# One adaLN transformer block on one Trainium2 core: a hand-set order for all engines, transposed attention output, modulation on the activations, K tiles of 112

## The chip, the cores and the metric

The kernel runs on one core of one Trainium2 chip. A core has five engines with a queue of instructions each: TensorE (PE in the profile; PEld is its weight load), VectorE (DVE), ScalarE (ACT), GpSimd (POOL) and SyncE (SP, which issues the DMA transfers). The engines here take up their instructions in the order of their queues (in VectorE's timeline of after, further down, a copy whose input was ready at 10.26 us waits behind other work until 11.7). The metric is the time of one execution on the device in microseconds (us). The profile gives the clock that TensorE was granted, as a share of full speed; in one kernel, e11 below, the span went from 210.8 us at a mean of 1.0 to 222.1 us at 0.927. A run is called slow when it is over 1.5% above the fastest of its kernel. Comparisons use fast runs.

## The reference, cut to what matters

S = 2048 tokens, D = 448, 16 heads of 28, MLP width 1792, bf16. Each token attends to 8 keys: itself and those 2, 4, ..., 14 positions back.

```python
sa, ca, ga, sb, cb, gb = silu(c) @ w_mod            # six vectors of 448
h = layernorm(x) * (1 + ca) + sa
q, k, v = h @ wqkv                                  # 16 heads of 28
logits = q . k[pos - 2*w], w = 0..7, masked below 0 # scale 28**-0.5
x = x + ga * ((softmax(logits) @ v) @ wo)
h = layernorm(x) * (1 + cb) + sb
x = x + gb * (gelu(layernorm(h) @ w1 + b1) @ w2 + b2)
```

As keys and queries differ by even numbers, both kernels treat even and odd tokens as two sequences of 1024 with a plain window of 8.

## The kernel before

The framework orders the instructions: the program states them stage by stage, and the framework's scheduler fills each engine's queue, with extra "order" edges where the program asks for them. Features are split into K tiles of 128 rows, the last one 64 real rows, a row of ones for the bias, and zeros up to 128. The attention output has queries on partitions, so it must be divided and then transposed:

```python
# attention_block: 18 blocks of 114 queries against 121 keys
pv  = 4 matmuls lhsT=hT[:, kt, k0:k0+BK], rhs=Wv[:, kt, :]        # V of the block
for half in range(2):                                            # 16 logit matmuls, K = 28
    nc.tensor.matmul(lt[0:BK, rr, ...], lhsT=kT[32*r:32*r+DH, ft, k0:k0+BK],
                     rhs=qT[32*r:32*r+DH, ft, q0:q0+BQ], tile_position=(32*r, 0))
    nc.scalar.activation(out=et_v[...], in_=lt[...], func=ACT.Exp, ...)
nc.vector.tensor_tensor(out=et, in0=et, in1=mask_rest, op=ALU.mult)
for h in range(H):                                               # et is the stationary side
    nc.tensor.matmul(po[0:BQ, h, :], lhsT=et[0:BK, h, :], rhs=vb[0:BK, h, :])   # 28 + a ones column
nc.vector.reciprocal(out=rden, in_=po[0:BQ, :, DH])
nc.vector.tensor_tensor(out=on, in0=po[..., 0:DH], in1=rden, op=ALU.mult)
for kt in range(KT):                                             # four transposes
    nc.tensor.transpose(out=pt[:, kt, :], in_=on[...], identity=ident[...])
nc.scalar.copy(out=oT[...], in_=pt[...])
# ... cut ...
# start: the modulation is folded into the weights
ca1_col = 1 + (silu(c) @ w_mod)[ca];  Wqk = wqkv * ca1_col;  Wv = wqkv * ca1_col
for ch in range(3):                                              # the bias sa @ wqkv
    4 matmuls lhsT=sa_pad[:, kt, :], rhs=wqkv_st[:, kt, ch*D:(ch+1)*D]
# ... cut ...
# order of the program
phases = [(range(0, 5), [0]), (range(5, 9), [1, 2]), (range(9, 14), [3, 4]),
          (range(14, 16), [5]), (range(16, 18), [6, 7])]         # attention blocks, MLP tile pairs
```

An MLP tile pair is 256 tokens: 56 W1 matmuls with 256 columns, Gelu, 28 W2 matmuls with 448 columns. Phases alternate attention (Exp on ScalarE) and MLP (Gelu), as each change of function costs a table load (1.28 us in the trace).

The softmax here doesn't subtract the row's maximum and nothing guards it: scores larger than these inputs give would overflow.

## Time and profile before

| | before |
|---|---|
| time, median of the runs (lowest to highest) | 238.4 us (237.66 to 239.23, four runs) |
| profiled span, mean granted clock | 234.2 us, 0.973 |
| TensorE, VectorE, ScalarE, GpSimd busy | 87%, 65%, 45%, 23% |
| start of the first QK matmul; end of QK for the first 512 tokens | 17.0 us; 25.4 us |
| TensorE time of the attention (V, logits, output, transposes) | 51.5 us |

The end of QK is taken as the start of its last matmul.

This is the profile page of before, first its span and busy times, then the rows of 40 slices for TensorE's busy share (9 is 90% or more) and for its granted clock (tenths of full speed), then the chain of waits by engine:

```profile
span 234.2 us, 4226 instructions
...
PE 204.8 (87%) x1712; PEld 130.6 (56%) x1712; DVE 151.4 (65%) x367; ACT 104.3 (45%) x139; POOL 54.4 (23%) x93
...
PE   0669988799978699989799998999998999899892
...
PEclk9997997999999999999999999799999999999998
...
PE 55%; DVE 23%; ACT 7%; POOL 6%; DMA 4%; issue 2%; SPq 1%; POOLq 0%; DVEq 0%; ACTq 0%
```

TensorE bounds the kernel. One caution for the clock: its record begins with the first change, at 13.6 us in before and 6.4 us in after, and the page counts the time before that as full speed. The spacing of matmuls says otherwise: before's bias matmuls (448 columns, 9.3 to 13.6 us) start 374 ns apart, where matmuls of 448 columns later start 189 ns apart. So the mean clocks quoted here leave out a slow start.

The next view is the timeline of TensorE in one attention block of before (start, duration of the group, engine, line, operation, out<-in, and in brackets the wait before it with what ended it):

```profile
97.49 0.32 PE L351 MATMUL lt<-qT,kT 28*121 28x114 bf16 x4
97.80 0.93 PE L383 MATMUL pw<-wo_s,oT 128*128 128x448 bf16 x4
98.67 0.44 PE L351 MATMUL lt<-qT,kT 28*121 28x114 bf16 x12
99.04 0.97 PE L340 MATMUL pv<-Wv,hT 128*121 128x448 bf16 x4
100.00 0.43 PE L351 MATMUL lt<-qT,kT 28*121 28x114 bf16 x8
100.36 0.40 PE L340 MATMUL pv<-Wv,hT 128*121 128x448 bf16 x1
100.83 0.43 PE L351 MATMUL lt<-qT,kT 28*121 28x114 bf16 x8
101.18 0.78 PE L340 MATMUL pv<-Wv,hT 128*121 128x448 bf16 x3
102.66 1.01 PE L366 MATMUL po<-vbuf_94,et 121*114 121x29 bf16 x16 [0.70 <-DVE et L361]
```

The output group (po) takes 0.87 us from start to start (15.6 us for 18 blocks).

Third, the start of before in the same view: the bias matmuls (pbias) and, last, the first QK group (pq), both after waits:

```profile
9.27 4.55 PE L259 MATMUL pbias<-wqkv_st,sa_pad 128*65 128x448 bf16 x12 [0.69 <-DMA wqkv_st<-in_A_wqkv_dram]
...
16.98 1.44 PE L198 MATMUL pq<-hT,Wqk 128*128 128x512 bf16 x3 [0.79 <-DVE hT L191]
```

Last, three groups of the page (count, then total busy us and mean ns of one): these weight loads of 114 and 121 columns take 132 to 136 ns each.

```profile
L366 PEld LDWEIGHTS <-et 121*114 121x114 bf16 x288 | 17.2, 133 | 7.4 <-DVE et L361 6.0
...
L351 PEld LDWEIGHTS <-kT 28*121 28x121 bf16 x288 | 11.1, 132 | 10.4 <-issue 9.6
...
L340 PEld LDWEIGHTS <-hT 128*121 128x121 bf16 x72 | 8.8, 136 | 3.4 <-issue 0.3
```

### The profile page before, as it was taken

The numbers are of one execution on the slowest core, as the hardware profiler recorded it, in microseconds if no ns is written. First come the engines' busy times: TensorE is split into PE (matmuls) and PEld (weight loads), VectorE is DVE, ScalarE is ACT, GpSimd is POOL, SyncE is SP. The second block draws the span as 40 slices with busy tenths as digits, with TensorE's granted clock in tenths as the row PEclk, the third lists the DMA queues.
The fourth block names the chain that finished last, engine by engine and source line by source line (L and its number), as shares of the span: only waits on it lengthen the run. The fifth ranks groups of instructions, "written<-read, shape, count | busy, mean of one in ns | idle before, by whom it ended". The sixth has DMA issues, their size and how long they took to land.

```text
span 234.2 us, 4226 instructions
## 1 busy us (share of the span) xinstructions
PE 204.8 (87%) x1712; PEld 130.6 (56%) x1712; DVE 151.4 (65%) x367; ACT 104.3 (45%) x139; POOL 54.4 (23%) x93
## 2 busy tenths in 40 slices
PE   0669988799978699989799998999998999899892
PEld 0433454365354376557686655787754675575660
DVE  5694979799978771578765557777556743666101
ACT  2324285325123158287357317655723364742230
POOL 8498000121112320023340003124202310213000
PEclk9997997999999999999999999799999999999998
DMA  6769980000001111001102200101112110200102
GB/s 203 218 200 331 351 271 3 0 0 0 3 0 22 22 28 22 3 0 25 22 0 48 78 3 0 22 3 22 27 22 78 25 22 3 78 13 9 25 0 78
DMA packets 17766, 13.37 MB, mean 57 GB/s; under 512 B 9042, under 2 KB 16851, under 8 KB 17748
## 3 DMA queue, kind: packets, MB, share of 16 engines
q1 hardware_dynamic: 17748, 13.12, 19.1%
q8 instruction: 13, 0.21, 0.4%
q14 instruction: 5, 0.04, 0.1%
HBM read 9.18 MB, written 1.84 MB: 47 GB/s over the span
## 4 chain that ended last, share of the span: by engine, by line
PE 55%; DVE 23%; ACT 7%; POOL 6%; DMA 4%; issue 2%; SPq 1%; POOLq 0%; DVEq 0%; ACTq 0%
PE pq L198 8%; PE po L366 5%; PE pw L383 4%; PE pv L340 3%; ACT hm L420 3%; PE lt L351 3%; DVE x_all L385 3%; DMA wqkv_st<-in_A_wqkv_dram 3%; DVE et L361 2%; POOL x1p_ring L393 2%; ACT et L357 2%; PE pbias L259 2%; DVE on L370 2%; DVE w_s L330 1%; PE pt L374 1%
## 5 line engine op out<-in xcount | busy, mean ns | idle before, releaser
L416 PEld LDWEIGHTS <-w_s 128*128 128x128 bf16 x448 | 43.2, 98 | 10.2 <-issue 3.2
L198 PE MATMUL pq<-hT,Wqk 128*128 128x512 bf16 x128 | 33.2, 406 | 5.6 <-ACT qT L202 2.0
L357 ACT ACTIVATE et<-lt 121x912 bf16<-121x912 f32 x36 | 32.0, 936 | 6.5 <-PE lt L351 5.6
L393 POOL TENSOR_TENSOR x1p_ring<-x_all,gbb_bc 128x448 f32<-128x448 bf16 x16 | 16.7, 1044 | 75.0 <-DVE x_all L385 72.5
L449 PEld LDWEIGHTS <-hm 128*128 128x128 bf16 x196 | 18.3, 98 | 15.4
L198 PEld LDWEIGHTS <-Wqk 128*128 128x128 bf16 x128 | 12.9, 102 | 22.8 <-issue 11.6
L376 ACT COPY oT<-pt 128x456 bf16<-128x456 bf16 (+1 forms) x18 | 9.7, 540 | 30.3 <-PE pt L374 30.2
L366 PEld LDWEIGHTS <-et 121*114 121x114 bf16 x288 | 17.2, 133 | 7.4 <-DVE et L361 6.0
L361 DVE TENSOR_TENSOR et<-et,mask_rest 121x1824 bf16<-121x1824 bf16 x18 | 19.6, 1099 | 2.5 <-ACT et L357 2.4
L340 PE MATMUL pv<-Wv,hT 128*121 128x448 bf16 x72 | 19.2, 370 | 0.1
L351 PEld LDWEIGHTS <-kT 28*121 28x121 bf16 x288 | 11.1, 132 | 10.4 <-issue 9.6
L351 PE MATMUL lt<-qT,kT 28*121 28x114 bf16 x288 | 15.4, 231 | 1.4 <-ACT et L357 0.8
L202 ACT CAST qT<-pq 128x512 bf16<-128x512 f32 x16 | 9.4, 586 | 14.7 <-PE pq L198 14.7
L383 PE MATMUL pw<-wo_s,oT 128*128 128x448 bf16 x64 | 15.0, 357 | 0.7 <-ACT oT L376 0.6
L385 DVE TENSOR_TENSOR x_all<-pw,x_all 128x448 bf16<-128x448 f32 x16 | 9.9, 618 | 6.7 <-PE pw L383 6.6
L204 DVE CAST kT<-pq 128x512 bf16<-128x512 f32 x16 | 10.9, 682 | 4.3 <-PE pq L198 4.2
L370 DVE TENSOR_TENSOR on<-po,rden 114x448 bf16<-114x448 f32 x18 | 11.0, 613 | 0.2
L340 PEld LDWEIGHTS <-hT 128*121 128x121 bf16 x72 | 8.8, 136 | 3.4 <-issue 0.3
L368 DVE RECIPROCAL rden<-po 114x16 f32<-114x16 f32 x18 | 4.6, 254 | 9.2 <-PE po L366 9.1
L420 ACT ACT_TABLE_LOAD x5 | 6.4, 1283 | 6.7 <-PE p_1015 L416 6.6
L374 PE MATMUL pt<-ident,on 114*128 114x114 bf16 x72 | 6.9, 219 | 2.8 <-DVE on L370 2.7
L383 PEld LDWEIGHTS <-oT 128*128 128x128 bf16 x64 | 5.4, 99 | 6.8 <-ACT oT L376 3.1
(434 smaller groups left out, 354.8 us busy)
## 6 DMA issues: line engine op xcount, KB each, us to landing
out_dram<-x_all SPq DMA_DIRECT2D x4, 448.0 KB, 2.7
w_s<-in_B_w_dram SPq DMA_DIRECT2D x1, 1568.0 KB, 13.2
wmod_325<-in_w_mod_dram SPq DMA_DIRECT2D x1, 1344.0 KB, 6.6
w_s<-in_B_w_dram SPq DMA_DIRECT2D x1, 1344.0 KB, 13.2
x_all<-in_A_x_dram SPq DMA_DIRECT2D x2, 448.0 KB, 3.4
x_all<-in_A_x_dram SPq DMA_DIRECT2D x1, 896.0 KB, 8.8
wmod<-in_w_mod_dram SPq DMA_DIRECT2D x1, 672.0 KB, 5.1
wqkv_st<-in_A_wqkv_dram SPq DMA_DIRECT2D x1, 672.0 KB, 6.3
```

The source lines that it names most:

```text
L198: nc.tensor.matmul(pq[:], lhsT=Wqk[:, kt, m, :], rhs=hT[:, kt, cc0:cc0 + 512], start=(kt == 0), stop=(kt == KT - 1))
L340: nc.tensor.matmul(pv[0:BK, :], lhsT=hT[:, kt, k0:k0 + BK], rhs=Wv[:, kt, :], start=(kt == 0), stop=(kt == KT - 1))
L351: mm = nc.tensor.matmul(lt[0:BK, rr, ft * BQ:(ft + 1) * BQ], lhsT=kT[32 * r:32 * r + DH, ft, k0:k0 + BK], rhs=qT[32 * r:32 * r + DH, ft, q ...
L357: ex = nc.scalar.activation(out=et_v[:, 2 * half:2 * half + 2], in_=lt[0:BK, :, 0:4 * BQ].rearrange("p r (ft c) -> p r ft c", ft=4), func= ...
L361: nc.vector.tensor_tensor(out=et[0:BK], in0=et[0:BK], in1=mask_rest[0:BK], op=ALU.mult)
L366: nc.tensor.matmul(po[0:BQ, h, :], lhsT=et[0:BK, h, :], rhs=vb[0:BK, h, :], start=True, stop=True)
L370: nc.vector.tensor_tensor(out=on[0:BQ].rearrange("p (h d) -> p h d", h=H), in0=po[0:BQ, :, 0:DH], in1=rden[0:BQ].unsqueeze(2).to_broadcast ...
L383: nc.tensor.matmul(pw[:], lhsT=oT[:, kt, jb * 128:(jb + 1) * 128], rhs=wo_s[:, kt, :], start=(kt == 0), stop=(kt == KT - 1))
L385: nc.vector.tensor_tensor(out=x1_blk(b), in0=pw[:], in1=x_all[:, b, :], op=ALU.add)
L393: nc.gpsimd.tensor_tensor(out=x1p_ring[:, b % NX1P, :], in0=x1_blk(b), in1=gbb2_bc[:], op=ALU.add)
L416: mm = nc.tensor.matmul(p1[:, f, :], lhsT=w1_s[:, kt, ft * 128:(ft + 1) * 128], rhs=yT[:, kt, :], start=(kt == 0), stop=(kt == KT - 1))
L449: nc.tensor.matmul(p2[:], lhsT=hm[:, ft, bi * 128:(bi + 1) * 128], rhs=w2_s[:, ft, :], start=(ft == 0), stop=(ft == FT - 1))
```

## The change

The intent is to keep TensorE fed. Four things change together.

**Order.** Every piece of work becomes a task with an engine, an assumed duration, the data it reads and writes, and the PSUM or SBUF buffers it holds. A list scheduler in the kernel's own Python code simulates the five queues; on each free engine it starts the ready task with the longest remaining dependency path (its rank). The resulting order is emitted as it is, with the framework's scheduler switched off.

```diff
+class Planner:
+    def plan(self):
+        for t in reversed(self.tasks):
+            tail = 0.0
+            for a in t.after:
+                lag = (DRAIN[t.eng] + SEM + t.late) if a.before[t] else 0.0
+                tail = max(tail, a.rank + lag)
+            t.rank = t.us + tail + t.rank_add
...
+            for e in ("PE", "DVE", "ACT", "POOL", "SP"):
...
+                    if best is None or (t.rank, -t.n) > (best.rank, -best.n):
+                        best = t
...
+    ctx.enter_context(tc.manual_schedule())
...
+    P.plan()
+    P.emit()
```

**Attention output transposed.** V (28 columns padded to 32) is now the stationary side and the exp weights move. Four column tiles work side by side, and the output arrives with features on partitions. The denominators come from four matmuls with ones, and their reciprocal from Ln and Exp on ScalarE. The four transposes, the copy to oT and VectorE's reciprocal go. 18 blocks of 114 queries become 17 of 121, and the key side is a full 128. The logits are issued as one group of 16 with four row tiles side by side, where before had two halves with two each:

```diff
-        for half in range(2):
-            for ft in range(4):
-                for rr in range(2):
-                    r = 2 * half + rr
+            for ft in range(4):
+                for r in range(4):
```

The output itself:

```diff
-        for h in range(H):
-            nc.tensor.matmul(po[0:BQ, h, :], lhsT=et[0:BK, h, :], rhs=vb[0:BK, h, :], start=True, stop=True)
-        nc.vector.reciprocal(out=rden[0:BQ], in_=po[0:BQ, :, DH])
-        ...multiply into on, four transposes, copy to oT...
+            for r in range(4):
+                nc.tensor.matmul(pd.t[HP * r:HP * r + HP], lhsT=ones_k[:, variant, :], rhs=et.t[:, r],
+                                 start=True, stop=True, tile_position=(0, HP * r))
+            for ft in range(4):
+                for r in range(4):
+                    nc.tensor.matmul(po.t[HP * r:HP * r + HP, ft, :], lhsT=vbuf.t[:, ft * 4 + r, :],
+                                     rhs=et.t[:, r, ft, 0:BQ], start=True, stop=True, tile_position=(0, HP * r))
+        ...lden = Ln(pd), rden = Exp(-lden) on ScalarE...
+            nc.vector.scalar_tensor_tensor(out=oT[:, :, o0:o0 + BQ], in0=po.t[:], scalar=DEN_SCALE,
+                                           in1=rden.t[:, :, 0:BQ], op0=ALU.mult, op1=ALU.mult)
```

**Modulation on the activations.** (1 + ca) and sa are applied when the transposed, normalized x is copied out of PSUM, so the weight scaling and the bias matmuls go. Q and K weights still need a copy that pads each head from 28 to 32 columns. The first 512 tokens are taken in two chunks of 256.

```diff
+            add("DVE", 0.07 + n / 960, lambda: nc.vector.tensor_scalar(
+                out=dst, in0=src(), scalar1=mod_col[:, KT + kt:KT + kt + 1], scalar2=mod_col[:, kt:kt + 1],
+                op0=ALU.mult, op1=ALU.add), reads=["sa", "ca"], writes=w, bufs=[ptr])
```

**K tiles of 112.** 448 is 4 x 112, so the zero rows go, and the bias of W1 sits in row 113 of the last tile.

```diff
-KT = 4
-KOFF_N = [0, 128, 256, 320]
+KT, KP = 4, 112
```

## The prediction

> **What bounds the kernel now.** TensorE. The page shows matmuls busy 87% of the 234.2 us span, DVE 65%, ACT 45%; the chain that ended last is 55% PE. Matmuls overlap, so I took start-to-start spacings from the trace in order of time: about 109 ns per W1 matmul (448, 49 us), 190 per W2 or out-projection matmul (42 + 12 us), 216 per QK matmul (28 us), 205-215 per V matmul, 51-58 per attention-output matmul, 25-50 per logit. Capped at these rates the stream is 182 us; some 45 us is PE waiting: 12 in the first 20 us, 16 between 20 and 80 us (QK groups waiting for ACT and DVE to empty PSUM, transposes for layernorm), the rest at phase changes and before the last MLP tile (pw at 208.8, next W1 at 218.2, chain of waits). Tail after the last matmul: 4.5 us.
>
> **What the change does.**
> 1. Attention on PE. V (32 columns) becomes stationary, exp weights moving, four column tiles side by side; four ones-matmuls give denominators. Before, per block: 16 matmuls (0.85 us) and four transposes (0.2); after, an estimated 0.5-0.6 in all. V and logit weights become full 128 columns (98 ns against 132-136 in the groups). The Trainium skill, "TensorE: Matmul & The Clock Gate", section "Weight-path perf modes", ties fast load to 128 weights; these durations agree. 18 blocks become 17. Together 41 us to about 31.
> 2. Start. Modulation goes onto h after transposing; bias matmuls (4.4 us from 9.3) and weight scaling leave the chain. First QK moves from 17.0 us to about 10: 7-8 us saved.
> 3. K of 112, not 128 with zero rows: no PE time, only memsets.
> 4. DVE loses the reciprocal (4.6) and weight scaling. ACT loses 18 copies of oT (9.7), gains 34 Ln/Exp passes over 488 columns (estimated 0.55 each, 19 us), hT evictions and one table load (11 against 10, 1.28 us each): from 104 to 120-127 us, below PE, but nearly as full where QK evictions share it.
> 5. Order. The list scheduler puts MLP work into waits. I expect waits after the start to fall from 33 us to 12-18. The layernorm chain of tile 15 (9.4 us now) is covered only by six microseconds of W1, so 2-3 us stay.
>
> **Sum (estimate).** Stream 169, of which 2 before the first QK; start 10; waits 15; tail 4.5: span about 196.5, plus the 4.5 between span and time: **200.5 us, range 192 to 210**. Faster by over 2%: 0.97; within 2%: 0.02; slower: 0.01. Of the gain about 8 us is the start, 10-13 attention, the rest order.
>
> **What would show each step.** First QK at 9-11 us. From first denominator matmul to the next PE work 0.5-0.65 us per block; V weight load near 98 ns. ACT busy 118-130 us, DVE 125-140. Order: PE gaps over 1 us rare after 20 us, one of 2-3 us before the last pair's W1.
>
> **What would make it wrong.** If column-tiled matmuls do not run side by side, attention saves nothing (+8 us). If the hand-set task times differ from the chip's, in-order queues hold ready work behind blocked work, most likely at 20-80 us (+5 to 10). If the scheduler fills almost all waits, 192 or less. First loads later than 8 us move the start one for one.

## More of the kernel before

"TensorE time" of a kind of work is the sum, over its matmuls, of the time from one matmul's start to the next matmul's start, each cut at 250 ns (420 ns for V's 448 columns), so that long waits are left out but slow issue is not.

The logits (lt) and V (pv) alternate in fragments. The 18 x 16 logit matmuls stand in 35 such runs over the kernel, about two per block. That is mostly the program's own doing: its loop makes two halves of 8, and each half has two row tiles side by side. Such a half takes 0.36 us (100.00 to 100.36), so a block's 16 logits take 0.7 us even in whole halves. TensorE changes 70 times between logits, which use a part of the array, and other work.

## The result, and the profile after

The changed kernel took 204.9 us in the median of four fast runs (204.03 to 206.68). A ratio is computed as the mean time of one kernel's fast runs over that of the other's of the same rounds, so it is not quite the ratio of the medians quoted. Here it is 0.860, with a 95% interval of 0.853 to 0.866: 14% faster. The profiled execution was the slowest of the four, 206.68 us with a span of 205.0 us.

| | before | after |
|---|---|---|
| span, mean granted clock | 234.2 us, 0.973 | 205.0 us, 0.965 |
| TensorE, VectorE, ScalarE busy us | 204.8, 151.4, 104.3 | 185.6, 130.5, 121.3 |
| first QK matmul; end of QK for 512 tokens | 17.0; 25.4 us | 12.6; 22.0 us |
| TensorE time of the attention | 51.5 us | 30.2 us |
| changes into or out of matmuls on a part of the array | 70 | 62 |

The page of after, the same lines as shown of before:

```profile
span 205.0 us, 4197 instructions
...
PE 185.6 (91%) x1704; PEld 113.6 (55%) x1704; DVE 130.5 (64%) x342; ACT 121.3 (59%) x176; POOL 46.3 (23%) x87
...
PE   7769977999799999999999996899998794999991
...
PEclk9958999999999999999999999999999999589999
...
PE 67%; DVE 10%; ACT 9%; DMA 5%; issue 3%; POOL 2%; SPq 1%; DVEq 0%; POOLq 0%; ACTq 0%
```

TensorE's part of the chain has grown from 55 to 67%. But the clock row has two dips to 5, at the third and the 35th slice, which a busy share does not show: a slow matmul counts as busy.

The timeline of TensorE in after, at two attention blocks in mid-kernel:

```profile
75.34 0.39 PE L607 MATMUL pd<-et,ones_k 128*32 128x488 bf16 x4
75.55 0.39 PE L611 MATMUL po<-et,vbuf_115 128*32 128x121 bf16 x16
75.88 0.39 PE L580 MATMUL lt<-qT,kT 28*128 28x122 bf16 x16
76.21 0.93 PE L567 MATMUL pv<-Wv,hT 112*128 112x448 bf16 x4
77.07 0.39 PE L607 MATMUL pd<-et,ones_k 128*32 128x488 bf16 x4
77.28 0.39 PE L611 MATMUL po<-et,vbuf_116 128*32 128x121 bf16 x16
```

Read the starts, not the durations. The denominators (pd) hold TensorE from 75.34 to 75.55, the output (po) to 75.88, so both take 0.54 us, where before's output group alone took 0.87 us. All 16 logit matmuls now stand together and take 0.33 us, where before's two halves took 0.36 us each. The weight loads of logits and V, from the page's groups, are now of 128 columns and take 93 and 98 ns:

```profile
L567 PEld LDWEIGHTS <-hT 112*128 112x128 bf16 x68 | 6.2, 98 | 6.2 <-issue 0.6
...
L580 PEld LDWEIGHTS <-kT 28*128 28x128 bf16 x272 | 4.4, 93 | 6.6 <-issue 6.2
```

The start of after, TensorE's timeline. The first QK group waits 1.85 us for a VectorE eviction of hT:

```profile
12.63 1.89 PE L503 MATMUL pq<-hT,Wqk 112*128 112x256 bf16 x8 [1.85 <-DVE hT L463]
```

VectorE's timeline of the same time says why. The modulation columns (mod_col) stand in its queue behind the statistics (bn_stats) of the second load of x, which landed at 10.5 us; TensorE had issued ps_col, which they copy, from 8.35 to 10.1 us:

```profile
10.55 1.15 DVE L382 BATCH_NORM_STATS2 st_all<-x_all 128x6 f32<-128x448 bf16 x2 [0.22 <-DMA x_all<-in_A_x_dram]
11.62 0.17 DVE L383 BATCH_NORM_AGGREGATE mv_102<-st_all 128x2 f32<-128x6 f32 x1
11.70 0.13 DVE L437 COPY mod_col<-ps_col 112x4 f32<-112x4 f32 x1
11.74 0.17 DVE L383 BATCH_NORM_AGGREGATE mv_102<-st_all 128x2 f32<-128x6 f32 x1
11.84 0.13 DVE L439 TENSOR_SCALAR mod_col<-ps_col 112x4 f32<-112x4 f32 x1
12.07 0.73 DVE L463 TENSOR_SCALAR hT<-ptr,mod_col 112x256 bf16<-112x256 bf16 x2
```

And the end of after, TensorE's timeline from the last out-projection (pw) to the W1 matmuls of the last two tile pairs:

```profile
171.45 0.93 PE L646 MATMUL pw<-wo_s,oT 128*128 128x448 bf16 x4 [0.91 <-DVE oT L626]
174.18 3.60 PE L696 MATMUL p_2571<-yT,w_s 112*128 112x256 bf16 x16 [1.80 <-DMA yT<-ybuf_112]
177.57 3.35 PE L696 MATMUL p_2593<-yT,w_s 112*128 112x256 bf16 x16
180.75 1.93 PE L696 MATMUL p_2616<-yT,w_s 112*128 112x256 bf16 x16
```

The same 16 matmuls take 3.4 and 3.2 us from start to start in the first two groups and 1.76 us in the third. The clock was granted at 0.5 from 173.66 to 180.49 us, two steps of 3.413 us.

The next table puts the prediction's sum beside the trace. "Other matmuls" are QK, W1, W2, out-projection, modulation and the layernorm's transposes after the first QK, each from its own start to the next start, cut at its full-clock spacing. What then is left of the span is waits, slow clock and slow issue together.

| term, us | before, trace | predicted | after, trace |
|---|---|---|---|
| first QK matmul starts | 17.0 | 10 | 12.6 |
| attention on TensorE | 51.5 | 31 | 30.2 |
| other matmuls | 136.5 | 136 | 136.6 |
| waits and slow clock | 24.8 | 15 | 21.3 |
| tail after the last matmul | 4.4 | 4.5 | 4.3 |
| span | 234.2 | 196.5 | 205.0 |

The predicted 136 is its stream of 169 less 2 before the first QK and less 31 of attention. Two terms are off, the start by 2.6 us and the waits by 6.3 us. The prediction's own book for before had 41 us for attention and 33 us of waits; the trace has about 10 us more in attention, which is the slow issue of logits and V, and 8 us less in waits.

### The profile page after: what moved, and what is told of

Its sections match the earlier page's. It is cut to its first block, busy times and chain, and to the rows that moved or that the text cites. A ratio compares the mean times of both kernels' runs of the same rounds, so it can differ in the third digit from the quotient of the medians.

```text
span 205.0 us, 4197 instructions
## 1 busy us (share of the span) xinstructions
PE 185.6 (91%) x1704; PEld 113.6 (55%) x1704; DVE 130.5 (64%) x342; ACT 121.3 (59%) x176; POOL 46.3 (23%) x87
## 4 chain that ended last, share of the span: by engine, by line
PE 67%; DVE 10%; ACT 9%; DMA 5%; issue 3%; POOL 2%; SPq 1%; DVEq 0%; POOLq 0%; ACTq 0%
PE pq L503 12%; PE pw L646 4%; DMA x_all<-in_A_x_dram 4%; ACT hm L702 3%; ACT et L590 2%; PE pv L567 2%; PE p_2571 L696 2%; PE lt L580 2%; PE pd L607 2%; DVE st_all L382 2%; PE p_2593 L696 2%; PE p_1617 L715 1%; DVE x_all L721 1%; PE p_1117 L715 1%; PE p_2468 L715 1%
## 5 line engine op out<-in xcount | busy, mean ns | idle before, releaser
L696 PEld LDWEIGHTS <-w_s 112*128 112x128 bf16 x448 | 44.7, 101 | 13.3 <-issue 2.3
L598 DVE TENSOR_TENSOR et<-et,mask 128x976 bf16<-128x976 bf16 x34 | 22.6, 664 | 24.5 <-ACT et L590 24.1
L400 POOL TENSOR_TENSOR rs_all<-tv_all,neg_half 128x1 f32<-128x1 f32 (+1 forms) x35 | 22.8, 660 | 61.7 <-DVE tv_all L397 61.6
L590 ACT ACTIVATE et<-lt 128x976 bf16<-128x976 f32 x34 | 32.7, 1010 | 3.2 <-PE lt L580 3.2
L503 PE MATMUL pq<-hT,Wqk 112*128 112x512 bf16 (+1 forms) x160 | 30.9, 348 | 1.9 <-DVE hT L463 1.9
L503 PEld LDWEIGHTS <-Wqk 112*128 112x128 bf16 x160 | 16.0, 101 | 14.1 <-issue 2.2
L382 DVE BATCH_NORM_STATS2 st_all<-x_all 128x6 f32<-128x448 bf16 x32 | 19.1, 617 | 2.2 <-DMA x_all<-in_A_x_dram 2.1
L646 PE MATMUL pw<-wo_s,oT 128*128 128x448 bf16 x64 | 14.3, 354 | 4.0 <-DVE oT L626 4.0
L567 PE MATMUL pv<-Wv,hT 112*128 112x448 bf16 x68 | 15.4, 353 | 0.6 <-ACT vbuf_116 L571 0.2
L626 DVE SCALAR_TENSOR_TENSOR oT<-po,rden 128x484 bf16<-128x484 f32 x17 | 11.1, 654 | 3.9 <-ACT rden L619 3.9
L619 ACT ACTIVATE rden<-lden 128x488 f32<-128x488 f32 x17 | 10.7, 627 | 0.3
## 6 DMA issues: line engine op xcount, KB each, us to landing
x_all<-in_A_x_dram SPq DMA_DIRECT2D x1, 896.0 KB, 12.8
```

The source lines that it names most:

```text
L382: add("DVE", 0.53, lambda: nc.vector.bn_stats(out=st_all[:, sl, :], in_=src()), reads=key, writes=[f"st{sl}"])
L400: lambda: nc.gpsimd.tensor_tensor(out=rs_all[:, which, b0:b0 + n], in0=tv_all[:, which, b0:b0 + n], in1=neg_half[:, 0:n], op=ALU.pow),
L503: nc.tensor.matmul(pq.t[:], lhsT=Wqk[0:KP, kt, m, :], rhs=hT[0:KP, kt, c0:c0 + n], start=(kt == 0), stop=(kt == KT - 1))
L567: nc.tensor.matmul(pv.t[:], lhsT=hT[0:KP, kt, k0:k0 + BK], rhs=Wv[0:KP, kt, :], start=(kt == 0), stop=(kt == KT - 1))
L590: ex = add("ACT", 0.87, lambda half=half: nc.scalar.activation(out=et.t[:, 2 * half:2 * half + 2], in_=lts[half].t[:, :, 0:4 * EQ].rearran ...
L598: nc.vector.tensor_tensor(out=ev, in0=ev, in1=mask[:], op=ALU.mult)
```

## The experiments

All runs stand against the kernel before on the same chip and in the same rounds; its median was 240.7, 239.2 and 240.5 us in the three sessions. Twelve kernels ran. Each result is given as the median of all runs and the ratio of the fast runs to before's; after itself has 0.860 [0.853, 0.866].

### What is the order worth, and what are the operations?

**e1_framework_order.** The new operations in the framework's order: no hand-set plan, tasks stated stage by stage as before's program did.

```diff
-    ctx.enter_context(tc.manual_schedule())
-    P.plan()
-    P.emit()
+    for t in sorted(P.tasks, key=program_stage):   # second half of an MLP pair after the next attention blocks
+        t.made = t.fn()
+        for e in t.only_order: tc.add_manual_dep(t.made[0].ins, e.made[-1].ins.name, SCHED, reason="order")
```

> The changed kernel's operations, tiles and buffers, but the engines' orders are left to the framework's own scheduler, as in the kernel before (phase-order hints kept, second MLP matmuls put after the next attention blocks, as before did). Theory: attention on TensorE and the start give about half of the gain, the hand-set order the other half, so this run takes 215 to 226 us, with more TensorE waiting at 20 to 80 us. Rival 1, the order is worth little: 204 to 209 us. Rival 2, the order is nearly all: 230 us or more.

Measured: 250.7 us (245.9 to 250.9), and the output was wrong (relative error 0.5). My edit delayed the second MLP matmuls so far that a ring of six residual tiles was overwritten before they were read. The engines did the same work, so the time is a hint that the rival (230 us or more) holds.

**e12_framework_order_right.** The same with a ring that is long enough, and a correct output.

```diff
-    NX1P = 6
+    NX1P = 10
```

> The run with the framework's order again, with a ring of 10 and not 6 tiles for the residual, which the delayed second MLP matmuls had overwritten (that made its result wrong). Expected correct, and about as slow: 240 to 252 us. The hand-set order would then be worth about 40 us for these operations, and the operations without it nothing against the kernel before. Rival, the wrong run was slow for its own reason: 215 to 226 us, as first expected.

Measured: median 250.0 us; one run was fast, 243.5 us at a clock of 0.918, the others slow, so there is no ratio. Its page (span, busy times, clock row), of one of the slow executions:

```profile
span 250.0 us, 4203 instructions
...
PE 213.4 (85%) x1704; PEld 124.3 (50%) x1704; DVE 140.1 (56%) x342; ACT 122.8 (49%) x176; POOL 45.3 (18%) x87
...
PEclk9769689769989985899598589999967999999998
```

The number of matmuls is that of after, 1704, yet the kernel is slower than before. Its fast run is 38 us above the mean of after's, 205.1. So the order is worth more than all new operations together, and the operations without it are worth nothing here. Two things show where it goes. The span less every matmul at its full-clock spacing is about 43 us more in this trace than in after's. And the clock: 59.5 us of this execution ran at 0.5, against 14.3 us in after and 12.4 in before. The clock fell again and again (the row of digits); in the 3.4 us before each of its seven falls after the start TensorE was busy for 28 to 56%. An estimate: half speed costs at most half of its stretch, so up to 23 of the 43 us are the clock. The fast run's mean of 0.918 over 241.8 us makes some 40 us at half clock. One limit: before's statement order had been tuned for the framework's scheduler, e12's had not, so 38 us is the distance to this order, not to the best one that the framework could make.

**e2_old_attention_output.** The old form of the output (et stationary, ones column, reciprocal, transposes, copy) in the hand-set order, planned anew.

```diff
-                    nc.tensor.matmul(po.t[HP * r:HP * r + HP, ft, :], lhsT=vbuf.t[:, ft * 4 + r, :],
-                                     rhs=et.t[:, r, ft, 0:BQ], start=True, stop=True, tile_position=(0, HP * r))
+                    nc.tensor.matmul(po.t[0:BQ, h, :], lhsT=et.t[:, r, ft, 0:BQ], rhs=vbuf.t[:, h, 0:DH + 1],
+                                     start=True, stop=True)
```

> Only the attention output is undone: exp weights stationary again, 29-column moving V with a ones column, reciprocal and multiply on DVE, four TensorE transposes and an ACT copy; still planned by the list scheduler. Theory: TensorE loses about 0.5 us per block (0.85 + 0.2 against 0.55), 17 blocks, so 8 to 10 us more: 212 to 216 us, with ACT about 10 us less busy. Rival, TensorE time in attention is hidden in waits anyway: 204 to 208 us.

Measured: 220.2 us, ratio 0.925 [0.918, 0.933], 15 us above after. With e12 this fills a table of TensorE time of the attention (same counting as above):

| | framework's order | hand-set order |
|---|---|---|
| old form | 51.5 (before) | 39.6 (e2) |
| new form | 45.4 (e12) | 30.2 (after) |

Two things have to be taken out before this table is read. First, the clock: e12 ran at half clock for a quarter of its span. Counted in full-clock stretches alone and scaled to all blocks, e12 has 40.6 us, before 50.9 and the other two what they had. The form is then worth 9 to 10 us, and for the new form the order is worth about 10. Second, the row of the old form does not show the order alone: e2 undoes the output, but keeps after's logit loop and 128-column loads. Of the 12 us between before and e2, 7.8 are logits (13.8 us in before, 6.0 in e2), and two whole halves of before's loop against one group of 16 (0.72 against 0.33 us per block, 7 us for 18 blocks) explain nearly all of it. No run has before's loop in the hand-set order. In e12, which has the new loop, the logits still take 14.3 us at full clock (6.6 in after): there the framework's order splits the groups of four, and TensorE waits before and inside them for Exp to free PSUM (12.8 us idle before logits in its page, 1.4 in after's). It changes 60 times between a part of the array and the whole, no more often than after with 62, so the number of changes is not the cause. Of e2's 15 us the attention explains 9.4. The rest is seen at one place of e2's timeline, a wait of 12 us for the layernorm of the tiles before the last pairs, which its own plan left open (W1 of that pair began at 174.2 us in after), with the clock at half from 179.7 to 193.4 us:

```profile
187.49 2.74 PE L697 MATMUL p<-yT,w_s 112*128 112x256 bf16 x12 [11.88 <-DMA yT<-ybuf]
```

So e2's total mixes the form with the luck of another plan; its attention time is the cleaner number.

### What happens at the end?

**e4_rank_of_last_pairs.** The plan gives rank by the longest dependency path and does not see that TensorE is shared. The layernorm chains of tiles 12, 13 and 14 so had equal rank and were interleaved on VectorE, and the W1 of pair 6 had to wait for both of its tiles. One term lifts that pair.

```diff
-            wm = add("PE", 0.435 * nf, mm, ..., bufs=[yT, p1], order_after=lts)
+            wm = add("PE", 0.435 * nf, mm, ..., bufs=[yT, p1], order_after=lts, rank_add=8.0 if j == 6 else 0.0)
```

> One number: the W1 tasks of the last pair but one get 8 us of rank, so that the layernorm of its two tiles (12, 13) goes ahead of that of tile 14 on DVE; TensorE's and ACT's orders stay but for a few neighbours. Theory: its W1, which waited until 174.2 us for the second transpose, starts 2 to 3 us earlier, TensorE's idle time before it stays under 1.5 us, the granted clock does not fall to half there (it did from 173.7 to 180.5 us, and 32 matmuls took 6.7 us and not 3.5), and the time falls by 4 to 6 us. Rival, the chain of tile 15 decides the end: time within 1 us.

Measured: 203.2 us (200.9 to 205.5), ratio 0.848 [0.840, 0.855]. TensorE's timeline at the end:

```profile
172.47 0.93 PE L646 MATMUL pw<-wo_s,oT 128*128 128x448 bf16 x4 [0.91 <-DVE oT L626]
174.03 6.34 PE L696 MATMUL p<-yT,w_s 112*128 112x256 bf16 x56 [0.64 <-DMA yT<-ybuf]
```

The wait before W1 went from 1.80 to 0.64 us, the clock did not fall, and 56 matmuls took 6.2 us where after's first 32 alone took 6.57. From the last out-projection to the end of the span it took 28.9 us against 33.5. The total gained less than these 4.6 us, about 2.9 (the difference of the ratios times 239). Between the two profiled executions the spans differ by 3.6 us: e4's was 0.7 us later when 512 tokens were done, and its clock fell once at 127 us. The rest is the spread of the runs, as after's profiled run was 1.6 us above its mean and e4's 1.0 us. This is the best version found; its interval and after's overlap at the edge.

**e5_keep_busy_at_end.** Waits left as they are, but useless matmuls on a tile of zeros put into them: 4 before the last out-projection, 8 before the W1 of pair 6. If the clock is the cost, this recovers it without shortening a wait.

```diff
+    for n, count in ((796, 4), (813, 8)):
+        at = [t.n for t in P.order].index(n)
+        P.order.insert(at, Task(-1, "PE", 0.0, lambda count=count: keep_warm(count), (), 0.0, 0.0))
```

> Twelve matmuls on a zero tile whose result nobody reads are put into TensorE's two waits before the last W1 groups: 4 before the last out-projection, 8 after it (0.86 and 1.7 us at full clock). All else as in the changed kernel. Theory: the fall of the granted clock to half at 173.7 us comes from TensorE having had little to do in the 3.4 us before it; with the filler the clock stays full, the first 32 W1 matmuls take 3.5 us and not 6.7, and the time falls by 2.5 to 3.5 us. Rival 1, the clock falls all the same (the time does not depend on activity): time the same or up to 0.5 us more. Rival 2, the filler delays real work: 1 us more.

Measured: 204.5 us, fast runs 202.0 to 203.3, ratio 0.851 [0.844, 0.859]. The timeline at the end:

```profile
176.22 1.89 PE L783 MATMUL pkeep<-warm_w 128*128 128x512 bf16 x8
178.27 6.33 PE L696 MATMUL p<-yT,w_s 112*128 112x256 bf16 x56 [0.16 <-DMA yT<-ybuf]
```

The first 32 of these W1 matmuls took 3.54 us. The end took 30.6 us, 3.0 us less than after, with no wait removed. So the fall of the clock costs 3.0 us there, and the waits themselves the remaining 1.6 us that e4 also won. Run e9 below confirms the 3.0 us with nothing edited at the end. The profiled execution was a slow one, so only the end segment is compared, where its clock was full.

### What happens at the start?

The prediction had the first QK at 10 us; it came at 12.6. Four edits tried to move it.

**e6_three_warmups.** Fewer warm-up matmuls at the very start, in case they delay the first real ones.

```diff
-NWARM = 12
+NWARM = 3
```

> Three warm-up matmuls in place of twelve, order unchanged. They end at about 2.6 us and not 6.5, so the condition vector's matmul and the silu chain go earlier by 3 us or more. Theory: nothing is won by this alone, because the modulation columns wait on DVE behind the layernorm statistics of the second x load, which landed at 10.5 us: first QK at 12.0 to 12.7 us, time within 0.7 us of the changed kernel. Rival, the silu chain is what bounds the start: first QK at 9 to 10.5 us, time 2 to 3 us less.

Measured: 205.2 us, ratio 0.863 [0.857, 0.870]; first QK 13.1, 512 tokens done at 22.6. The warm-ups neither help nor hurt by much. This trace lacks the clock's record before 17.4 us, but the spacing of matmuls settles it: QK matmuls of 256 columns start 213 ns apart until then, against 109 ns afterwards, so the clock was at half. The modulation matmuls (ps_col) began 1.3 us sooner than in after, at 7.09 us, and ended at the same time, 10.24 us, since they started 93 ns apart and not 52. So the edit did not shorten the chain to the first QK, and the expected 3 us did not come.

**e7_stats_behind_modulation.** The statistics of the second x load moved behind the first hT evictions in VectorE's queue, the order of the rest untouched.

```diff
+    late = [t for t in P.order if t.n in (91, 92, 93, 94, 95, 96)]
+    rest = [t for t in P.order if t not in late]
+    at = [t.n for t in rest].index(66) + 1
+    P.order = rest[:at] + late + rest[at:]
```

> The layernorm statistics of tiles 2 and 3 on DVE (and their Ln and Exp on ACT) are put behind the first hT evictions, in the order of the two queues; nothing else. Theory: the modulation columns are then copied when their matmuls end (10.2 us), first QK at 10.8 to 11.3 us and not 12.6, time 1 to 1.5 us less. Rival, what is won there is lost again at the second chunk, whose statistics are now later: time within 0.5 us.

Measured: 206.9 us, ratio 0.869 [0.864, 0.874]. TensorE's timeline:

```profile
11.30 1.88 PE L503 MATMUL pq<-hT,Wqk 112*128 112x256 bf16 x8 [0.60 <-ACT hT L467]
14.38 1.19 PE L489 MATMUL ptr<-ident,zbuf 128*112 128x128 bf16 x8 [1.20 <-DVE zbuf L405]
```

The first QK did start 1.3 us sooner, so the queue was what held it. But the second chunk's transposes now wait for the normalization that was pushed back. TensorE stands idle at 13 to 14.4 us, and the clock stayed at half from 9.9 to 20.2 us (after: 9.8 to 16.65). The 512 tokens were done at 23.8 us, 1.8 us later than in after. The gain was paid back with interest at the next wait.

**e8_both_at_start.** e6 and e7 together.

```diff
+NWARM = 3, and the six tasks moved as in e7
```

> Three warm-ups and the statistics behind the modulation, both of the edits before. Theory (two waits in a row, each hiding the other): first QK at 8.8 to 9.8 us, a gain at the first QK of 3 us or more, larger than the sum of the two alone; time 2 to 3 us less than the changed kernel, unless the second chunk, which waits for the second x load at 10.5 us, takes it back. Rival, loads of the QK weights bound it: first QK not before 10.5 us.

Measured: 207.6 us, ratio 0.872 [0.865, 0.880]; first QK 11.35, 512 tokens at 24.0. No earlier than e7 alone. Two things end together here. With 3 warm-ups the modulation matmuls run at the slow spacing, as in e6; the first line is TensorE's timeline of e8, the second that of after:

```profile
7.09 3.15 PE L432 MATMUL ps_col<-silu_bf,wm_st 112*112 112x1 bf16 x32 [0.19 <-DMA wm_st<-in_w_mod_dram]
...
8.35 1.91 PE L432 MATMUL ps_col<-silu_bf,wm_st 112*112 112x1 bf16 x32
```

And the copies of the key weights, whose load landed at 10.06 us, stand before mod_col in VectorE's queue. So the rival (not before 10.5 us) holds, but whether the loads or the slow clock held the first QK was not separated.

**e9_keep_busy_at_start.** Zero-tile matmuls in the waits of the start: 4 before the first transposes, 9 before the first QK.

```diff
+    for n, count in ((64, 4), (81, 9)):
+        ...insert keep_warm(count) ahead of task n, as in e5...
```

> The changed kernel with 13 matmuls on the zero tile put into TensorE's two waits before the first QK matmul: 4 before the first transposes, 9 before QK. Nothing is won on the loads or on DVE, so the first QK stays at 12.6 to 13.3 us. Theory: QK starts at half clock because the waits before it let the clock fall (at 9.8 us in the changed kernel, until 16.7); with the filler the clock is full when QK starts or within 1 us of it, QK of the first 512 tokens ends at 19.8 to 20.7 us and not at 22.0, and the time falls by 1 to 2 us. Rival, the low clock at the start is a ramp that activity does not change: end at 22 us, time the same.

Measured: 206.6 us, ratio 0.872 [0.865, 0.880]; first QK 14.0, 512 tokens at 21.5. The filler put the first QK off by 1.4 us, and the start became only 0.5 us shorter at the 512-token point; the clock still fell at 10.3 us, for one window and not two, though TensorE was busy for 98% of the 3.4 us before, and it fell again from 30.8 to 37.6 us. At the end nothing had been edited, yet in this run the clock did not fall there:

```profile
176.55 6.34 PE L696 MATMUL p<-yT,w_s 112*128 112x256 bf16 x56 [1.80 <-DMA yT<-ybuf]
```

The first 32 W1 took 3.54 us, and the end took 30.5 us, as in e5. In e6, e7 and e8, with the same end, the clock fell for one window of 3.4 us and the end took 32.1 to 32.2 us; in after it fell for two and took 33.5. So the same waits need not cost the clock: it depends on how they fall into the windows, which the Trainium skill calls free-running (see below).

### Are K tiles of 112 worth anything?

**e3_k_tiles_of_128.** Three K tiles of 128 rows and one of 64, with after's plan on all engines.

```diff
-KT, KP = 4, 112
+KO = [0, 128, 256, 384]
+KR = [128, 128, 128, 64]
```

> Same plan and same order on every engine; only the contraction of 448 is cut 128+128+128+64 (without zero rows) and not 4 x 112, so the weight loads write 128 partitions and not 112. Theory: the 112-partition loads are slow by themselves (about 290 KB/us in the first 20 us, against about 400 in the kernel before), so here the rate returns to 350 to 400 KB/us, the second x load lands about 2.5 us earlier, the first QK matmul starts at 11.0 to 11.5 us and not 12.6, and the time falls by 1 to 2 us. Matmul spacings do not change. Rival, the rate is a matter of the order of the loads and not of their shape: rate and first QK unchanged, time within 0.5 us.

Measured: 225.1 us (217.8 to 226.9), mostly slow runs, so no ratio: its clock was half from 10.8 to 34.7 us in the profiled run. The total does not tell whether the tiles cost time or only the lost clock, so the same tiles were run on a version with a busier start. (The trace does tell: after 34.7 us, at full clock, a QK matmul of 512 columns took 263 ns from start to start, against 217 in after. So the expected "matmul spacings do not change" failed. The first QK, at 11.6 us, nearly came as expected.)

**e10_combined.** The version without the K change: e4's rank, e7's move, two QK groups ahead of the second chunk's transposes, and small fillers at start and end.

```diff
+    put((91, 92, 93, 94, 95, 96), 66)
+    put((75, 77), 89)
+    for n, count in ((64, 4), (81, 3), (102, 3), (796, 4), (813, 3)): ...insert keep_warm(count)...
+    ..., rank_add=8.0 if j == 6 else 0.0
```

> All that the runs pointed to: rank for the last pair but one, filler at the end and at the start, statistics of tiles 2 and 3 behind the modulation, and two QK groups of the first 256 tokens ahead of the transposes of the next. Theory: the gain at the start, which the low clock took back when the statistics alone were moved (QK of the first 512 tokens then ended at 23.8 us), is kept when TensorE stays busy: that point at 18.5 to 20 us; the low clock lasts under 8 us in all; 198 to 201 us. Rival, the pieces do not add, since each shifts the free-running clock windows: 202 us or more.

Measured: 205.2 us, ratio 0.864 [0.855, 0.872]. The end took 29.1 us as in e4, but 512 tokens were done at 22.9 us, later than in after, so the parts do not add up to a better kernel than e4 alone.

**e11_combined_k128.** e10 with e3's tiles.

```diff
-KT, KP = 4, 112
+KR = [128, 128, 128, 64]
```

> The combined kernel with the K tiles of 128+128+128+64. These loads were faster (325 against 282 KB/us between 3 and 9 us), but alone the kernel was much slower because the clock stayed at half until 34.7 us. Theory: with the filler the clock rises by about 17 us and this kernel is as fast as the combined one or up to 1.5 us faster. Rival, the slow run had a cause of its own in the 128-row layout, not the clock's phase: 210 us or more again.

Measured: 217.4 us, fast runs 212.2 to 213.8, ratio 0.898 [0.889, 0.907]. In the profiled run the clock was full from 5.3 us, where its record begins, to the last matmul (mean 0.999), and the span was still 210.5 us. So the tiles have a cost of their own, as the rival said. TensorE's timeline shows two QK groups of 512 columns, first in e11:

```profile
56.84 2.21 PE L514 MATMUL pq<-hT,Wqk 128*128 128x512 bf16 x8
```

The same eight matmuls in after:

```profile
51.14 1.89 PE L503 MATMUL pq<-hT,Wqk 112*128 112x512 bf16 x8
```

From start to start one such matmul took 263 ns in e11 on average, against 217 in after and 221 in before (where the zero rows fill the last tile to 128). The single spacings say where: about 220 to 227 ns among tiles of 128 rows, 310 ns into and out of the tile of 64. That is 0.18 us for each group of four; V groups went from 0.76 to 0.95 us. W1, whose last tile has 65 rows with the bias, kept its 109 to 111 ns. The Trainium skill, page "TensorEngine Tiling (Array Packing)", section "Key Properties", says that changing the tiling mode, not just the tile, drains TensorE. The trace agrees with it, if a 64-row operand counts as another mode and a 65-row one as the full array: about 90 ns per change. An estimate from these numbers, 40 QK, 17 V and 4 modulation groups at 0.18 us, gives 11 us; the difference of the ratios of e11 and e10 times 239 us is 8 us. The estimate leaves out the transposes, which took 116 ns each and not 62, and the 8 us is measured although e11's fast runs had the better clock (means of 0.984 to 1.0, e10's 0.971 to 0.986); so the tiles probably cost more than 8 us.

The 128-row loads came a little faster: between 3 and 9 us the DMA moved 355 KB/us in before, 325 in e3 and 307 in e11, and 282 in after (255 to 297 in the other kernels of 112 rows). That suggests that 112-partition loads are slower, but the kernels' queues differ and no run isolates it, so this stays open.

## Why the prediction was right or wrong

The total was right: 200.5 us with a range of 192 to 210 was said, 204.9 was measured, and faster by over 2%. Inside it several steps held and several did not.

**Attention on TensorE: held.** "Together 41 us to about 31": after has 30.2 us. The denominator and output groups take 0.54 us per block (0.5 to 0.65 said), V's weight load 98 ns. The Trainium skill, page "TensorE: Matmul & The Clock Gate", section "Part 3: Packing small matmuls — row/col tiling", says that small matmuls at different tile positions run concurrently. The trace agrees: 16 output matmuls start about 12 ns apart. Its section "Weight-path perf modes" ties the fast load to 128 weights, and the groups agree with 93 to 98 ns against 132 to 136.

**The cause named for it: only half right.** The starting point of 41 us was too low, as it counted capped issue times: the trace has 51.5. The missing 10 us stood in the book as waits. In fact they were slow issue: of the logits, mostly by the loop that put two row tiles side by side, which the prediction did not count as part of the change, and of V, whose groups alternated with them. The gain came to 21 us where 10 were said: 10 from output and transposes (19.9 to 9.7 us by this count), 7 from logits, 4 from V. With e2 and e12, at full clock, the form is worth 9 to 10 us and, for the new form, the order about 10 us of the attention alone.

**The split of the gain: wrong.** "About 8 us is the start, 10-13 attention, the rest order." The start gave 4.4 us at the first QK and 3.4 us when 512 tokens are done. And e12 shows the terms are not independent: with the new operations and without the new order the kernel takes 244 to 252 us, more than before. The order was the condition for all the rest.

**The start: the step that failed.** "First QK moves from 17.0 us to about 10": it started at 12.6. The removed bias matmuls and weight scaling did leave the chain. What was missed is VectorE's queue, in which the modulation columns stood behind statistics whose data came at 10.5 us. e7 shows that, and also that it could not simply be undone, since the second chunk needs those statistics. Behind it stand loads and a slow clock (e8), which no run separates. The second x load is queued behind the Q and K weights; loading it sooner was not tried, so what the start could reach is open.

**The waits: mis-sized.** "Waits after the start to fall from 33 us to 12-18": by the trace's balance they went from 24.8 to 21.3 us, so 15 was 6.3 us too low. About 4.5 us of the 21.3 is not waiting at all but the clock at half speed, for which the sum had no term. At the end, 32 W1 matmuls took 6.57 us where they take 3.54 at full clock; at the start QK lost about 1.5 us. The waits that TensorE's view lists after the first QK are some 10 us; a remainder of some 6 us is short gaps that no run isolated.

**Why the clock fell: shown at the end.** The skill's page on the clock gate, section "Part 1: The HAM clock gate (the 'warmup' mystery)", describes a free-running window of 3413 ns and two states, half and full. All falls in these traces last multiples of 3.413 us at 0.5, but for those that the end of the record cuts. In after TensorE was busy for 1.22 us (36%) of the window from 170.25 to 173.66 us, then lost the next two. e5 fills the waits and recovers 3.0 us; e4 shortens them and recovers the same and 1.6 us more; in e9 the same waits lay so that the window had 47%, and nothing was lost. Over all 14 traces, cut into windows of 3.413 us in step with the trace's own clock changes: after a full-speed window with TensorE busy for under 44% the clock fell in 25 of 25 cases, between 44 and 70% in 15 of 56, above in 8 of 688 (before's fall at 37.5 us followed a window of 100%). So a low busy share went with a fall without exception, but there is no sharp threshold above it; what made the falls after busy windows was not tested.

**The wait at the end: right size, wrong tile.** "One of 2-3 us before the last pair's W1": the wait is 1.80 us, before the last pair but one, because tiles of equal rank were interleaved. Waits over 1 us are rare elsewhere, as predicted (they begin at 30.7, 53 and 125.5 us; one of 0.91 us at 170.5).

**Span to time: wrong.** The prediction added 4.5 us between span and time. It seems to have set the profile of one execution against the median of others (234.2 and 238.4 us). Measured on the same execution, the difference is 1.7 to 1.8 us in after's runs and at most 2.1 in any other.

**The rest held.** ScalarE was busy 121.3 us (118 to 130 said), VectorE 130.5 (125 to 140), and the other matmuls stayed at 136.5 us with K tiles of 112 ("no PE time"). That last point holds against the zero-filled tiles of before; against an unfilled tile of 64 rows, K = 112 is worth 8 us or more.

So the total was right by errors that partly cancel. The span came out 8.5 us over the predicted 196.5: the start +2.6, waits and clock +6.3, all else together -0.4. Against that stand 2.8 us less between span and time, and 1.8 us because the median run was shorter than the profiled one. From the prediction's own terms, 196.5 and 4.5 (it wrote 200.5 for this 201.0), that leads to the measured 204.9 us.

## What to carry to other kernels

When TensorE bounds a kernel, count its time from start to start by kind of work: slow issue looks like busy time, and small matmuls gain from a loop that puts more tiles side by side as well as from an order that keeps their groups whole. Look at the granted clock beside the busy share, since waits of 1 to 2 us that follow closely can cost as much again in the matmuls after them (0.91 and 1.80 us of waits, then 3.0 us lost). Where the trace lacks the clock's record, the spacing of like matmuls shows it. When an in-order queue holds early work behind late data, moving it is only a gain if what is pushed back has slack, so measure at the next point where everything must be ready.

## What the Trainium skill lacked or had wrong

- Page "TensorE: Matmul & The Clock Gate", table "Why this matters for your kernels": it warns of TensorE idle gaps over about 3 us. Here the clock fell after waits of 0.91 and 1.80 us with a short group between them, 1.22 us of a window of 3.413 us busy. Below a busy share of 44% it fell in 25 of 25 windows, so one gap is not what decides. The page does name short idles between groups elsewhere (section "A second HAM failure mode: psum-queue depth-cycling"), but gives no share for them.
- The same page, section "Part 1: The HAM clock gate (the 'warmup' mystery)": it puts the ramp penalty below 1% of a typical span. For QK at the start of after that fits, 1.5 of 205 us. The falls later in the kernel come on top and are what it leaves out: 3.0 us at the end of after, and in e12 59.5 us of 250 at half clock in all.
- Page "TensorEngine Tiling (Array Packing)", section "Key Properties": it says that a change of mode drains TensorE, with no figure. Elsewhere it advises row tiling for a contraction of 64, but has no word that a plain matmul with a 64-row operand already brings a change about. Here a 64-row K tile among 128-row tiles cost 0.18 us per group of four (310 ns against 220 to 227 for a spacing); 65 and 112 rows cost nothing visible.
- Pages "DMA: Bandwidth & Descriptors" and "SBUF — State Buffer": the first says how many engines share a load of another shape (its rule gives all 16 for 112 partitions), the second has measured rates for ranges of 4 to 128 partitions; neither has one for 112. Loads to 112 partitions moved 282 KB/us in after between 3 and 9 us (255 to 297 in the other kernels), and those to 128 partitions 307 to 355; whether the partition count is the cause is open.
- Page "TensorE: Matmul & The Clock Gate", section "Part 1: The HAM clock gate (the 'warmup' mystery)": it says that the number of slow matmuls varies from run to run with the window's phase, but has no figure for how far the mean clock and the time of one kernel, on one core, spread. Here e11 had spans of 210.8 us at a mean clock of 1.0 (counted from the record's start), 212.1 at 0.984, 219.2 at 0.946 and 222.1 at 0.927. All profiled executions show only the page's two states, 0.5 and 1.0.
